# A new order of steps for a kernel whose TensorE plays attention and a gated network from one written list

## The chip, the cores and the metric

One core of a Trainium2 chip runs the whole program. The metric is the device time of one execution in microseconds; the time before is 1254.93, the median of three runs (1253.8 to 1256.23).

## The reference

The input x has 2048 tokens of 512 features. Two branches are computed from it and mixed by a gate for each token. All arrays are float32.

```python
g = sigmoid((x * gate_w).sum(-1, keepdims=True))

# branch A: attention, 32 query heads of 16, one shared key and value head
q = (x @ wq).reshape(B, S, 32, 16).transpose(0, 2, 1, 3)
k, v = x @ wk, x @ wv
p = softmax(einsum("bhqd,bkd->bhqk", q, k) * 16 ** -0.5)
a = einsum("bhqk,bkd->bhqd", p, v).transpose(0, 2, 1, 3).reshape(B, S, 512) @ wo

# branch B: a gated network of width 1376
b = (gelu(x @ w_gate) * (x @ w_up)) @ w_down

out = g * a + (1 - g) * b
```

## The kernel before

**Tiling.** The tokens are cut into 4 groups (`NTG`) of 512 (`TG`); the width 1376 into 11 chunks (`NF`) of up to 128; keys and values into 16 chunks (`NKC`) of 128 tokens. The 32 heads are handled in units of 4: a unit `u` is 4 heads for one group of 512 queries, so there are 32 units of 16 key chunks, 512 steps (`nsteps`). Two units make one block of heads, four blocks (`NB`) one group. Weights and activations are split into a high and a low part (names ending in h and l), and each product is made of three: high by high, low by high, high by low.

A first part, which the change doesn't touch, loads x, projects the queries (written to a scratch array `scr` in HBM and read back as `Q`), the keys (`kp`) and the values (`v1`, `v2`), and does the first chunks of the network. It ends about 82 us into the span.

**The list.** From there on TensorE's order is written out by hand. `PLAN` is a list of 78 strings, called entries here and counted from 0 (entry 0 stands on line 45). Each names a queue of jobs and a word of steps, and `play` emits them one after the other:

- `S`: `score`, one half of a step's scores. Two matmuls (L751) fill a pair of PSUM banks, and one exponential on ScalarE (L754) writes them to `p`, of which there are 12 (`PB`). There are three pairs of banks; `S` takes the one of the first two that was used longest ago, so it waits for the exponential that last read it. `Z` is the same step with the third pair, which it shares with the job's tile `z`.
- `V`: `visit`, one step of probabilities by values: eight matmuls in the trace (L821) into `acc`, from two tiles `p`. Behind the sixteenth V of a unit, `norm` is called: VectorE copies the sums (L765 or L775), and the normalization of a block (L781 to L799: two sums, a shuffle, four reciprocals, a product, and the split into `oh` and `ol`) is put into a list `bg`.
- `H`: begins a job; `z` and `y` are its two PSUM tiles. `F`: one pair of products, one for `z` and one for `y`, side by side on 64 rows each (L519). `R`: ends the job.
- `T`: queues the tanh of the job's GELU on ScalarE; the rest of the GELU follows on VectorE two and three scores later.

A job goes through its products twice, with the two halves of the rows exchanged in the second round; the hand-over from one half to the other waits for a small memset on GpSimd (`mark`, L527), which waits for the last products of the first half.

**The jobs.** Queue `f` holds the network's: a `gate_job` (12 products, so 24 F) makes gate and up projection of one chunk and starts its GELU; a `down_job` multiplies two or three chunks by `w_down` for two rows of 128 tokens and adds to `acc`. Behind the last chunk of a group, `reload_x` fetches x for the next one in four chunks; they are split when a slot in `pair_mm` comes up, and what is left is flushed when the next gate job begins (DVE casts on L201, GpSimd subtracts on L202). Queue `w` holds six output projections (`wo_job`): two for each of the first three groups, 12 products each, three for each of the four blocks of heads in order. When one begins, it flushes `bg`, so that the pending normalization is put into VectorE's queue:

```python
def begin():
    flush(lazy)
    flush(bg)
    return [[t for bl in range(NB) for t in wo_terms(g, k, bl)] for k in (i, i + 1)]
```

Each engine runs its own instructions in the order in which they were emitted and waits for the others by semaphores. `defer` and `run_later` tie the emission of small work (loads of Q, splits of weights) to the count of scores.

Of the kernel before, what the change touches and what calls it, by code (L numbers as in the profile page):

```python
# [20 lines left out]
S = 2048  # L21
D = 512
H = 32
DH = 16
F = 1376
# [16 lines left out]
EVERY = 3  # L42
PB = 12
PLAN = [
# [78 lines left out]
]  # L123


# [811 lines left out]
```

## Time and profile before

| | |
|---|---|
| median of three runs | 1254.93 us |
| the profiled execution | 1252.53 us |
| its span, first to last instruction | 1250.5 us |
| mean granted TensorE clock | 0.998 |
| ScalarE busy | 1033.1 us (83%) |
| VectorE busy | 521.1 us (42%) |
| GpSimd busy | 215.5 us (17%) |

TensorE's busy time counts overlapping matmuls up to their modelled ends, so it is near the whole span whether TensorE is fed well or not; the starts of its instructions tell more. Each instruction of the profile is named by its engine, its line, and its tiles, output before input: `acc<-p,v` reads `p` and `v` and writes `acc`. Engines are PE (TensorE), PEld (its weight loads), DVE (VectorE), ACT (ScalarE), POOL (GpSimd) and SP (which issues loads).

### The profile page before, as it was taken

Reading aid. Unit: us, or ns where it says so; the run is one execution under the profiler, and the core shown is the slowest. Engines: PE = TensorE matmul, PEld = TensorE weight load, DVE = VectorE, ACT = ScalarE, POOL = GpSimd, SP = SyncE. Lnnn points to the kernel's source line nnn. Section 1 sums busy time; section 2 is a strip of 40 time slices with the busy share of each in tenths; the row PEclk is TensorE's granted clock in tenths of the full one; section 3 lists DMA queues with packets and bytes.
Section 4 is the critical chain, followed back from the end, with each engine's and each line's share of the span. In section 5 each row is a group of like instructions: output and inputs, shape, how many; then the busy total and the mean of one; then the engine's idle time right before and its main releaser. Section 6 shows DMA issues by size and latency. Waiting matters only on the chain.

```text
span 1250.5 us, 23618 instructions
## 1 busy us (share of the span) xinstructions
PE 1240.0 (99%) x9742; PEld 657.4 (53%) x9742; DVE 521.1 (42%) x844; ACT 1033.1 (83%) x1127; POOL 215.5 (17%) x265
## 2 busy tenths in 40 slices
PE   9999999999999999999999999999998999999998
PEld 6865455454555554454455554455554555554444
DVE  7862453524423342533434253242635125253334
ACT  5448888889888889888988888987886888988894
POOL 5420312112210120211230021120331011121100
PEclk9999999999999999999999999999999999999999
DMA  8540302112200211201220111110220201011000
GB/s 328 194 153 38 94 1 65 40 48 82 73 15 24 75 40 40 65 23 47 74 72 19 57 65 40 40 40 23 85 82 14 73 14 65 14 52 40 14 1 34
DMA packets 28317, 73.89 MB, mean 59 GB/s; under 512 B 4208, under 2 KB 4464, under 8 KB 28208
## 3 DMA queue, kind: packets, MB, share of 16 engines
q1 hardware_dynamic: 27664, 71.32, 17.2%
q8 instruction: 77, 1.26, 0.4%
q0 software_dynamic: 256, 0.79, 0.2%
q10 hardware_dynamic: 288, 0.26, 0.1%
q14 instruction: 32, 0.26, 0.1%
HBM read 57.41 MB, written 14.94 MB: 58 GB/s over the span
## 4 chain that ended last, share of the span: by engine, by line
PE 92%; DVE 1%; DMA 0%; SPq 0%; ACT 0%; issue 0%; DVEq 0%
PE acc L821 38%; PE s L751 23%; PE y L519 16%; PE z L519 14%; PE wos L504 1%; DVE nz L787 0%; DMA Q<-scr 0%; DVE acc L634 0%; PE wof L504 0%; DVE sq L547 0%; DVE n L778 0%; DVE gs L555 0%; DVE sq L554 0%; DVE nt L790 0%; DVE sq L548 0%; DVE hl L560 0%
## 5 line engine op out<-in xcount | busy, mean ns | idle before, releaser
L754 ACT ACTIVATE p<-s 128x1024 f32<-128x1024 f32 x1024 | 979.8, 1025 | 157.5 <-PE s L751 142.7
L821 PE MATMUL acc<-p,v 128*32 128x512 f32 x4096 | 498.1, 600 | 0.0
L751 PE MATMUL s<-Q,kp 51*128 51x512 f32 x2048 | 396.9, 421 | 1.5 <-DMA Q<-scr 1.5
L751 PEld LDWEIGHTS s<-Q,kp 51*128 51x128 f32 x2048 | 183.4, 184 | 260.5 <-ACT p L754 158.4
L821 PEld LDWEIGHTS acc<-p,v 128*32 128x32 f32 x4096 | 107.3, 109 | 235.6 <-issue 224.0
L527 POOL MEMSET mark<- 1x1 f32 x77 | 7.7, 100 | 869.8 <-PE y L519 857.7
L544 DVE COPY gs<-z 128x512 f32<-128x512 f32 x39 | 27.0, 691 | 250.8 <-PE z L519 225.9
L519 PE MATMUL z<-xh,gh 64*128 64x512 f32 x312 | 123.2, 395 | 0.0
L519 PE MATMUL y<-xh,gh 64*128 64x512 f32 x312 | 123.1, 395 | 0.0
L519 PE MATMUL z<-xl,gh 64*128 64x512 f32 x312 | 121.9, 391 | 0.0
L519 PE MATMUL y<-xh,gl 64*128 64x512 f32 x312 | 121.9, 391 | 0.0
L519 PE MATMUL y<-xl,gh 64*128 64x512 f32 x312 | 121.9, 391 | 0.0
L519 PE MATMUL z<-xh,gl 64*128 64x512 f32 x312 | 121.9, 391 | 0.0
L202 POOL TENSOR_TENSOR gl<-st,gh 128x512 fp32r<-128x512 f32 x80 | 107.0, 1355 | 60.9 <-DVE gh L201 48.7
L624 DVE SCALAR_TENSOR_TENSOR acc<-z,gc,acc 128x512 f32<-128x512 f32 x24 | 18.0, 751 | 144.2 <-PE z L519 115.3
L519 PE MATMUL z<-dh,hh 64*128 64x512 f32 x176 | 69.4, 395 | 0.0
L519 PE MATMUL y<-dh,hh 64*128 64x512 f32 x176 | 69.4, 394 | 0.0
L519 PE MATMUL y<-dl,hh 64*128 64x512 f32 x176 | 68.9, 391 | 0.0
L519 PE MATMUL z<-dh,hl 64*128 64x512 f32 x176 | 68.8, 391 | 0.0
L519 PE MATMUL z<-dl,hh 64*128 64x512 f32 x176 | 68.8, 391 | 0.0
L519 PE MATMUL y<-dh,hl 64*128 64x512 f32 x176 | 68.8, 391 | 0.0
L519 PEld LDWEIGHTS z<-xh,gh 64*128 64x128 f32 x312 | 58.1, 186 | 8.1 <-issue 1.7
(174 smaller groups left out, 1534.8 us busy)
## 6 DMA issues: line engine op xcount, KB each, us to landing
st<-wf SPq DMA_DIRECT2D x40, 768.0 KB
scr<-q SPq DMA_DIRECT2D x16, 512.0 KB
Q<-scr SPq DMA_DIRECT2D x64, 128.0 KB
Q<-scr SPq DMA_DIRECT2D x64, 64.0 KB
out<-acc SPq DMA_DIRECT2D x16, 256.0 KB
xr<-xT SPq DMA_DIRECT2D x6, 512.0 KB
xst<-xT SPq DMA_DIRECT2D x12, 256.0 KB
st<-wf SPq DMA_DIRECT2D x5, 256.0 KB
```

The costliest lines, as they stand in the source:

```text
L202: eng_l.tensor_sub(lo, src, hi)
L504: nc.tensor.matmul(ps, a, b, start=(first and q == 0), stop=(last and q == len(terms) - 1), skip_group_check=True)
L519: mm = nc.tensor.matmul(ps, a[rs], b[rs], start=(half == 0 and q == 0), stop=(half == 1 and q == len(X) - 1), skip_group_check=True)
L527: relay = nc.gpsimd.memset(mark, 0.0).ins
L544: nc.vector.tensor_copy(gs, g)
L624: nc.vector.scalar_tensor_tensor(o, ps, w, o, op0=ALU.mult, op1=ALU.add)
L751: nc.tensor.matmul(ps[:, j * TG : (j + 1) * TG], kp[rs, kc * P : (kc + 1) * P], Q[u][rs, pr], start=True, stop=True)
L754: nc.scalar.activation(p, ps, AF.Exp, bias=0.0, scale=SCALE)
L821: nc.tensor.matmul(accp[u][32 * j : 32 * j + 32], vt[:, kc], pb[s, j // 2][:, (j % 2) * TG : (j % 2 + 1) * TG], start=(kc == 0), stop=(kc ...
```

## The change

Only the strings of `PLAN` differ. There are 78 entries before and after, with the jobs in the same order: the three pairs of output projections are entries 22 and 23, 41 and 42, 60 and 61 in both. Between them the numbers of scores, values and the places of `Z` and `T` are dealt out anew. The first entry, the entries around the output projections and the last ones, of 78 that nearly all differ:

```diff
 PLAN = [
-    "t: S",
-    "f: H F S F5 S F4 S F2 S V S F2 S F4 S F4 S F2 R S V Z S T S V3 S Z S V2 S",
...
-    "f: H F3 S F5 S F S V2 S2 F6 S F3 R S V S Z S V2",
-    "f: H F2 S F4 S F3 S V S F3 S F3 S F3 R S V2 Z S2 V3 S",
-    "w: H F2 S F4 S F3 S F3 S V S F2 S F4 S F3 S F3 R S V Z S2 V2 S Z V2 S2 Z V3 S",
-    "w: H F S F5 S F3 S F3 S V2 S2 F6 S F3 S F3 R S V2 Z S2 V2",
...
-    "f: H F5 S F S V S F3 S F3 R S V Z S2 V3 Z S2 V2 S",
-    "f: H F3 S F3 S V S F2 S F4 R S V S Z S V2 S",
-    "f: H F3 S F4 S F4 S F S V3 S2 F6 S F3 S F3 R S V S Z T S V2 Z S V2 S",
-    "f: H F4 S F2 S F6 S2 F6 S F5 S F R S V3 T Z S2 V2",
-    "f: H F S F2 S F4 S F2 S V S F3 S F3 S F3 R S V S Z S V3 S",
-    "w: H F S F5 S F6 S2 V3 S F3 S F3 S F4 S F2 R S V2 S Z S V2 S",
-    "w: H F3 S F4 S F2 S F3 S V4 S F S F5 S F3 S F3 R S V Z S2 V2 S",
...
-    "f: H F3 S F3 S F4 S F2 S V2 S F S F5 S F3 S F3 R S V3 T S Z S V2 S",
-    "w: H F4 S F4 S F2 S F2 V S F2 S F4 S F4 S F2 R S V S Z S V3 S Z S V3 S",
-    "w: H F S F5 S F3 S F3 S V3 S F2 S F4 S F4 S F2 R S V2 S2",
...
-    "f: H F3 S F3 S V S F2 S F4 R S V S Z S V2 S V3",
+    "t: S2",
+    "f: H F6 S F3 S F3 S V S F S F5 S F3 S F3 R S V S Z T S V2 Z S V2 S",
...
+    "f: H F3 S F3 S F3 S V S F2 S F4 S F3 R S V Z S2 V4 S Z S V2 S",
+    "f: H F3 S F5 S F S V S F3 S F3 S F3 R S V Z S2 V2 Z S V S Z V2 S2 Z V3 S",
+    "w: H F3 S F3 S F4 S F2 S V S F2 S F4 S F3 S F3 R S V Z S2 V3 S Z S V2 S",
+    "w: H F3 S F3 S F4 S F2 S V3 S F S F5 S F3 S F3 R S V Z S2 V3 S",
...
+    "f: H F3 S F3 S V S F S F5 R S V S Z S V2 S",
+    "f: H F4 S F2 S V S F6 R S2 V3 S",
+    "f: H F S F5 S F3 S F3 S V S F S F5 S F3 S F3 R S V Z S T S V4 S Z S V2 S",
+    "f: H F3 S F3 S F4 S F2 S V S F3 S F3 S F3 S F3 R S V Z S T S V4 Z S2 V2 S",
+    "f: H F3 S F5 S F S V S F3 S F3 S F3 R S V Z S2 V2 Z S V S Z V S2 V3 S",
+    "w: H F S F5 S F3 S F3 S V S F S F5 S F4 S F2 R S V2 S",
+    "w: H F S F5 S F4 S F2 S V4 S2 F6 S F3 S F3 R S V S Z S V2 S",
...
+    "f: H F4 S F3 S F5 S2 F6 S F3 S F3 R S V2 Z T S2 V4 S",
...
+    "f: H F2 S F4 S F4 S F2 S V S F3 S F3 S F3 S F3 R S V Z S V2 T S Z S V2 Z S V2 S Z S V2 S",
+    "w: H F3 S F3 S F3 S F3 S V S F S F5 S F5 S F R S V2 S Z S V4 S2",
+    "w: H F6 S F5 S F S V2 S2 F6 S F4 S F2 R S V2 S2",
...
+    "f: H F3 S F3 S V S F2 S F4 R S V Z S2 V2 S V3",
 ]
```

120 rows, old and new, of the table PLAN are left out of this document.

## The prediction

> **What bounds the kernel now.** I read the page first (busy shares, chain, groups), then the waits, then TensorE's timeline gap by gap.
>
> ```profile
> PE 1240.0 (99%) x9742; PEld 657.4 (53%) x9742; DVE 521.1 (42%) x844; ACT 1033.1 (83%) x1127; POOL 215.5 (17%) x265
> PE 92%; DVE 1%; DMA 0%; SPq 0%; ACT 0%; issue 0%; DVEq 0%
> L754 ACT ACTIVATE p<-s 128x1024 f32<-128x1024 f32 x1024 | 979.8, 1025 | 157.5 <-PE s L751 142.7 <-DMA Q<-scr 6.7 <-ACT p L754 1.1
> L751 PEld LDWEIGHTS s<-Q,kp 51*128 51x128 f32 x2048 | 183.4, 184 | 260.5 <-ACT p L754 158.4 <-issue 31.0 <-DVE gs L544 15.1
> ```
>
> TensorE is the bound: 92% of the chain that ended last. ScalarE has 157.5 us of idle time before its exponentials, most of it waiting for scores. The change only reorders TensorE's steps, so its price has two parts: what a step costs by its neighbours, and where TensorE waits. The prices, from the middle of the run (S = one score step, L751; F = one pair of products z and y, L519; V = one value step, L821, eight matmuls):
>
> ```profile
> 620.67 0.39 PE L519 MATMUL y<-dh,hl 64*128 64x512 f32 x1
> 620.90 0.40 PE L751 MATMUL s<-Q,kp 51*128 51x512 f32 x2
> 621.23 1.06 PE L821 MATMUL acc<-p,v 128*32 128x512 f32 x8
> 622.23 0.50 PE L751 MATMUL s<-Q,kp 51*128 51x512 f32 x2
> 622.57 0.39 PE L519 MATMUL y<-dh,hh 64*128 64x512 f32 x1
> 622.80 0.39 PE L519 MATMUL y<-dl,hh 64*128 64x512 f32 x1
> 623.03 0.40 PE L751 MATMUL s<-Q,kp 51*128 51x512 f32 x2
> 624.20 0.50 PE L751 MATMUL s<-Q,kp 51*128 51x512 f32 x2
> 624.63 1.07 PE L821 MATMUL acc<-p,v 128*32 128x512 f32 x8
> 626.51 1.92 PE L821 MATMUL acc<-p,v 128*32 128x512 f32 x16
> 628.37 0.50 PE L751 MATMUL s<-Q,kp 51*128 51x512 f32 x2
> ```
>
> From start to start: F to S, F to F and S to F 0.23; S to V 0.33 (620.90 to 621.23); one V 1.00, two 1.86 (626.51 to 628.37); the S behind a V 0.34.
>
> Where TensorE waits, there is one large place, at entry 60 of the list (counted from 0), the third pair of output projections. Its columns: start, length, engine, line, operation, and in brackets the idle time and what ended it.
>
> ```profile
> 951.06 0.39 PE L519 MATMUL z<-xh,gl 64*128 64x512 f32 x1
> 951.28 0.40 PE L751 MATMUL s<-Q,kp 51*128 51x512 f32 x2
> 951.61 2.78 PE L821 MATMUL acc<-p,v 128*32 128x512 f32 x24
> 954.33 0.96 PE L751 MATMUL s<-Q,kp 51*128 51x512 f32 x6
> 955.22 1.92 PE L821 MATMUL acc<-p,v 128*32 128x512 f32 x16
> 957.07 0.50 PE L751 MATMUL s<-Q,kp 51*128 51x512 f32 x2
> 959.74 0.40 PE L519 MATMUL y<-woh,ol 64*128 64x512 f32 x1
> 964.09 0.50 PE L519 MATMUL z<-woh,oh 64*128 64x512 f32 x1 [3.96 <-DVE oh L795]
> 967.11 0.79 PE L751 MATMUL s<-Q,kp 51*128 51x512 f32 x2
> 969.08 0.39 PE L519 MATMUL y<-woh,oh 64*128 64x512 f32 x1
> 951.49 0.69 DVE L544 COPY gs<-z 128x512 f32<-128x512 f32 x1 [1.10 <-PE z L519]
> 957.34 0.75 DVE L781 SCALAR_TENSOR_TENSOR nz<-n,mk,nz 128x512 f32<-128x512 f32 x1
> 963.61 0.43 DVE L795 CAST oh<-nt 128x512 fp32r<-128x512 f32 x1
> 961.00:964.00 3.00, 0.00 (x0) 0.00 (x0) 2.93 (x5) 0.02 (x1) 0.00 (x0) 1.00 0.00 0
> 965.30:968.60 3.30, 3.30 (x18) 1.34 (x18) 0.00 (x0) 1.25 (x2) 0.09 (x1) 0.50 0.00 0
> 969.00:972.00 3.00, 3.00 (x32) 2.17 (x30) 0.17 (x1) 2.65 (x4) 0.00 (x0) 1.00 0.00 0
> ```
>
> The tenth product of the job is the first that reads the last head block (oh, written by the cast at 963.61). It should start 0.23 behind 959.74, at 959.97, and starts at 964.09: 4.12 lost. In the windows (the seventh number behind the colon's stretch is the granted clock) TensorE does nothing from 961 to 964, and its clock then is 0.50 from 965.3 to 968.6 and 1.00 again from 969. The steps from 964.09 to 969.08, F S F F V S F F S F F, cost 3.28 by the prices above and took 4.99: another 1.7. So this one place costs 5.8 us.
>
> **The change part by part.** The job counts are equal: 1608 F, 1024 scores (904 S and 120 Z before, 905 and 119 after), 512 V, 77 jobs, 39 T. No instruction is added or removed; the part before the list and the tail behind it are untouched.
>
> *1. The wait at entry 60.* VectorE normalizes the block behind the GELU chain of entry 59's job, in the order of its queue, whatever TensorE does: from the copy at 951.49 to the end of the cast, 964.04. The new list keeps block 23's last V in the same place, in the middle of entry 59, but puts much more behind that entry's products. Before: S V3 S Z S V2 S, then 9 F and 2 S to the tenth product: 8.9 us from 951.06 to the 959.97 that it would be without the wait. After: S V Z S V2 S Z S V2 Z S V2 S Z S V2 S, then 9 F and 3 S. By the prices: V 1.00 + 4 x 1.86 = 8.44; twelve scores, five of 0.33 (in front of a V), five of 0.34 (behind one), and two of 0.23 in between, 3.81; 0.23 into the first; 12 x 0.233 = 2.8. Sum 15.3, so TensorE comes 6.4 later. VectorE comes later too: T, which queues the tanh, stands behind three scores instead of one, so two more exponentials can stand ahead of it on ScalarE.
>
> ```profile
> 623.12 2.86 ACT L754 ACTIVATE p<-s 128x1024 f32<-128x1024 f32 x3 [0.70 <-PE s L751]
> ```
>
> One exponential is 1.025 alone and three back to back 2.86, so (2.86 - 1.03)/2 = 0.915 each in a queue: 1.8 us for two. Wait left: 4.12 + 1.83 - 6.4 = -0.4, none. Without an idle stretch the clock stays at 1.00, so the 1.7 goes with it. Taken: -5.8. If VectorE is a microsecond later than I walk it, some 0.6 of wait stays and the clock stays up. Next late there: nothing on VectorE; the other two pairs (entries 22 and 41) had no wait, and 22 too gets more V in front.
>
> *2. Fewer turns to V.* Three V take 2.72 (951.61 to 954.33), so a V is worth 0.86 and a run of them 0.14 more; with 0.10 for the S to V step (0.33 against 0.23) and 0.11 for the S behind it, each run costs 0.35 over its V. Runs of one, two, three, four V: 112, 108, 48, 10 before (278), 106, 117, 36, 16 after (275). 3 x 0.35 = -1.0. The hand-overs between S and F go up from 1007 to 1015 and cost nothing, since both ways are 0.23.
>
> [...]
>
> *3. The score banks.* At 624.20 a score starts 0.05 behind the end of the first exponential of the row quoted (623.12 + 1.03 = 624.15), and the V behind it comes 0.43 later, not 0.33: its bank came free about 0.15 after the exponential's end. The same delay, read off the gaps, stands in 16 places by 0.05 to 0.10 each, 1.1 us in all, of which the first and the last are:
>
> ```profile
> 124.82 0.49 PE L751 MATMUL s<-Q,kp 51*128 51x512 f32 x2
> 125.23 1.07 PE L821 MATMUL acc<-p,v 128*32 128x512 f32 x8
> 1204.59 0.46 PE L751 MATMUL s<-Q,kp 51*128 51x512 f32 x2
> 1204.88 0.39 PE L519 MATMUL y<-xh,gl 64*128 64x512 f32 x1
> ```
>
> In the new list short gaps between scores get rarer: F runs of two and four (which alternate) go from 77 and 79 to 59 and 56, of three from 240 to 268. Walking both lists with 0.915 per exponential and a release at 0.15, I find about one such place left in the new one (entry 50, where the halves meet at S2). Bounds: 0 if they only move, -1.6 if smaller delays go as well. Taken: -1.0.
>
> *4. The second reload of x, entry 38.* One new wait. The casts of its third and fourth chunk are queued at the job's begin, and in the new list the copy of a finished block (L765) is queued just ahead.
>
> ```profile
> 622.36 0.69 DVE L765 COPY n<-acc 128x512 f32<-128x512 f32 x1 [5.92 <-PE acc L821]
> 622.97 0.42 DVE L201 CAST xh<-xst 128x512 fp32r<-128x512 f32 x1
> 623.47 1.30 POOL L202 TENSOR_TENSOR xl<-xst,xh 128x512 fp32r<-128x512 f32 x1 [2.19 <-DVE xh L201]
> 628.80 1.47 POOL L202 TENSOR_TENSOR xl<-xst,xh 128x512 fp32r<-128x512 f32 x1 [1.29 <-DVE xh L201]
> ```
>
> The copy starts 1.13 behind its V (621.23), in the new list 0.2 ahead of the job's first F (V to S 0.97, S to F 0.34). From that F at 0: copy to 0.5, cast, GpSimd's subtraction from 1.0 to 2.3, the second to 3.6 or 3.8. The eighth F reads the first at 9 x 0.233 = 2.1, the eleventh the second at 3.0: waits 0.2 and 0.4, sum +0.6. Bounds 0 (earlier casts) to +1.4 (both subtractions at 1.47, casts as late). GpSimd's mark for the halves queues behind these and is needed only after a V (0.9 or more); no cost. SP's loads are asked for by the same calls in the same order; 8 us lie between the last reload's issue and its use, and no row shows a wait of TensorE for them behind the first score.
>
> Sum: -5.8 - 1.0 - 1.0 + 0.6 = -7.2. The profiled execution took 1252.53 (span 1250.5 and 2.0 around it), which gives 1245.3; it lies 2.4 under the median of the three runs, so the forecast is 1254.93 - 7.2 = 1247.7.
>
> **The rivals.**
> - The wait at entry 60 only shrinks, because tanh, the added copy or a cast slowed by GpSimd push VectorE 2 us further: -7.2 + 2.0 = -5.2, 1249.7. For it: my margin is 0.4. Against: two exponentials is already the worst order. Chance 0.12.
> - The new list doesn't do there what it seems to: VectorE's chain follows TensorE, and the whole wait with the slow clock stays: -1.4, 1253.5, no change. Against: the cast at 963.61 ends a VectorE stretch that has no gap but the one for tanh. Chance 0.06.
> - [...] Chance 0.03.
> - Slower: ScalarE. In 13 jobs instead of 7 the tanh is followed by three scores at once. If there the queue is behind by one whole exponential beyond the release, the third score waits 0.915 for its bank each time: 13 x 0.915 = +11.9, so +4.7, 1259.6. It decides once ScalarE is over two exponentials behind at T. Against: before, at 954.33, three scores follow a T and take 0.89, the unhindered 0.34 + 0.23 + 0.33, and ScalarE idles 157.5 us. Chance 0.05.
>
> **How the numbers follow.** Forecast 0.74. Its ends: -5.8 - 1.3 - 1.6 + 0 = -8.7 and -4.1 (1.7 of the wait left) - 0.7 - 0 + 1.4 = -3.4, so 1246.2 to 1251.5; with 0.7 for the scatter of a median of three runs (they span 1253.8 to 1256.23), 1245.5 to 1252.2, which takes in the first and third rival and leaves 0.11 and the tails out. What a measurement of this kernel can tell from no change is about 0.2%, 2.5 us: faster 0.89 (forecast, first and third rival), same 0.06, slower 0.05.
>
> **What would show it.** In the profile after: no idle time of some 4 us for DVE oh among the waits; granted clock 1.00 through the whole list; 0.2 to 0.8 us of waiting for xl at about 623 to 625 us; V runs at the same 1.00, 1.86, 2.72; fewer S to V gaps over 0.40. Wrong if TensorE idles at entry 60, if a half-speed window appears elsewhere, or if scores behind T wait.

## The result, and the profile after

The new list takes 1247.15 us (median of six runs, 1245.13 to 1247.75) against 1254.28 for the old one measured beside it. The ratio is 0.9941 (95% interval 0.9928 to 0.9953), so 6 to 9 us less. The forecast was 7.2 us less, 1247.7. The profiled execution took 1246.9 with a span of 1244.8; before it was 1252.53 with 1250.5.

The page after, busy shares, chain and the two groups that answer to those of before:

```profile
PE 1237.2 (99%) x9742; PEld 657.5 (53%) x9742; DVE 526.2 (42%) x844; ACT 1031.7 (83%) x1127; POOL 215.6 (17%) x265
PE 92%; issue 1%; POOL 0%; DVE 0%; ACT 0%; DMA 0%; SPq 0%; POOLq 0%
L754 ACT ACTIVATE p<-s 128x1024 f32<-128x1024 f32 x1024 | 977.4, 1026 | 150.3 <-PE s L751 139.7
L751 PEld LDWEIGHTS s<-Q,kp 51*128 51x128 f32 x2048 | 183.7, 184 | 258.0 <-ACT p L754 167.3
```

Nothing in these lines tells where 6 us went: the shares are the same to a percent, and weight loads even wait longer for ScalarE in total (167.3 against 158.4), although the list is shorter. The timeline tells. At entry 60, the rows of TensorE and one of its weight loads, those of VectorE and ScalarE, and two windows:

```profile
952.09 0.39 PE L751 MATMUL s<-Q,kp 51*128 51x512 f32 x2
952.41 1.06 PE L821 MATMUL acc<-p,v 128*32 128x512 f32 x8
953.40 0.73 PE L751 MATMUL s<-Q,kp 51*128 51x512 f32 x4
966.59 0.39 PE L519 MATMUL z<-woh,ol 64*128 64x512 f32 x1
966.59 0.19 PEld L751 LDWEIGHTS s<-Q,kp 51*128 51x128 f32 x2
966.82 0.40 PE L751 MATMUL s<-Q,kp 51*128 51x512 f32 x2
967.05 0.39 PE L519 MATMUL z<-woh,oh 64*128 64x512 f32 x1
954.16 0.69 DVE L548 SCALAR_TENSOR_TENSOR sq<-sq,gs 128x512 f32<-128x512 f32 x1
956.50 0.69 DVE L554 SCALAR_TENSOR_TENSOR sq<-sq,gs 128x512 f32<-128x512 f32 x1 [1.65 <-ACT sq L551]
965.35 0.43 DVE L795 CAST oh<-nt 128x512 fp32r<-128x512 f32 x1
954.01 1.94 ACT L754 ACTIVATE p<-s 128x1024 f32<-128x1024 f32 x2 [0.41 <-PE s L751]
955.83 0.63 ACT L551 ACTIVATE sq<-sq 128x512 f32<-128x512 f32 x1
954.00:964.00 10.00, 10.00 (x84) 3.10 (x82) 8.11 (x14) 9.37 (x11) 0.00 (x0) 1.00 0.01 2
964.00:968.00 4.00, 4.00 (x34) 3.06 (x34) 2.40 (x4) 4.00 (x5) 0.00 (x0) 1.00 0.00 0
```

The cast that writes the last head block ends at 965.78; the tenth product starts at 967.05, when its turn comes, 1.27 us behind it. TensorE is busy in all of both windows and its clock is 1.00. A V alone costs 1.00 (952.41 to 953.40) and 0.32 lies between the score and it, as before.

At entry 38 TensorE's rows with those of VectorE and GpSimd behind them, and the wait as the waits view groups it (idle time of the weight loads: us in total, times, longest):

```profile
623.54 0.40 PE L519 MATMUL z<-xh,gh 64*128 64x512 f32 x1
625.42 0.40 PE L519 MATMUL z<-xh,gh 64*128 64x512 f32 x1
625.90 0.50 PE L519 MATMUL z<-xl,gh 64*128 64x512 f32 x1
626.25 0.39 PE L519 MATMUL z<-xh,gl 64*128 64x512 f32 x1
626.71 0.39 PE L519 MATMUL z<-xh,gh 64*128 64x512 f32 x1
627.33 0.50 PE L519 MATMUL z<-xl,gh 64*128 64x512 f32 x1 [0.24 <-POOL xl L202]
623.33 0.69 DVE L765 COPY n<-acc 128x512 f32<-128x512 f32 x1 [0.73 <-PE acc L821]
623.94 0.75 DVE L201 CAST xh<-xst 128x512 fp32r<-128x512 f32 x2
624.44 2.84 POOL L202 TENSOR_TENSOR xl<-xst,xh 128x512 fp32r<-128x512 f32 x2 [5.88 <-DVE xh L201]
PEld z L519 <- POOL xl L202: 1.2, 2, 0.7
```

The gaps are 0.48 and 0.62 where 0.23 is usual, and the step behind the first is 0.35 (625.90 to 626.25): the matmul that had waited also held up the next here, by 0.12.

The whole list, from its first score to the last run of V:

```profile
82.24 0.93 PE L751 MATMUL s<-Q,kp 51*128 51x512 f32 x4 [0.95 <-DMA Q<-scr]
1226.74 2.78 PE L821 MATMUL acc<-p,v 128*32 128x512 f32 x24
```

That is 1144.50 us, against 1150.87 before (81.61 to 1232.48): 6.4 less. The first score came 0.6 later in this profile, from before the list; over all profiled executions told of here it lies between 81.4 and 83.2, whatever the list.

### The profile page after: what moved, and what is told of

Its sections match the earlier page's. It is cut to its first block, busy times and chain, and to the rows that moved or that the text cites. A ratio compares the mean times of both kernels' runs of the same rounds, so it can differ in the third digit from the quotient of the medians.

```text
span 1244.8 us, 23618 instructions
## 1 busy us (share of the span) xinstructions
PE 1237.2 (99%) x9742; PEld 657.5 (53%) x9742; DVE 526.2 (42%) x844; ACT 1031.7 (83%) x1127; POOL 215.6 (17%) x265
## 4 chain that ended last, share of the span: by engine, by line
PE 92%; issue 1%; POOL 0%; DVE 0%; ACT 0%; DMA 0%; SPq 0%; POOLq 0%
PE acc L821 38%; PE s L751 23%; PE y L519 17%; PE z L519 13%; PE wos L504 1%; POOL xl L202 0%; DVE acc L634 0%; DMA Q<-scr 0%; PE wof L504 0%; ACT p L754 0%; SPq L364 0%; ACT sq L551 0%; SPq L363 0%; POOLq L202 0%; POOL mark L527 0%
## 5 line engine op out<-in xcount | busy, mean ns | idle before, releaser
L751 PEld LDWEIGHTS s<-Q,kp 51*128 51x128 f32 x2048 | 183.7, 184 | 258.0 <-ACT p L754 167.3
L519 PEld LDWEIGHTS y<-xh,gl 64*128 64x128 f32 x312 | 57.7, 185 | 8.4
```

The lines of the kernel that those rows point to most:

```text
L519: mm = nc.tensor.matmul(ps, a[rs], b[rs], start=(half == 0 and q == 0), stop=(half == 1 and q == len(X) - 1), skip_group_check=True)
L751: nc.tensor.matmul(ps[:, j * TG : (j + 1) * TG], kp[rs, kc * P : (kc + 1) * P], Q[u][rs, pr], start=True, stop=True)
```

## The experiments

The base of e1 and e2 is the old list, that of the others the new one. "List" is the time from the start of the first score to the start of the last V in the trace: 1152.6 before, 1146.2 after. Times in brackets are ranges of runs, ratios are to the old kernel. Distances to the new list are those of the medians; the ratios, made with other runs of the old kernel, give some 0.5 us more for e3, e5 and e6.

**e1, the wait alone, taken out of the old list**

```diff
-    "f: ... R S V3 T S Z S V2 S",
-    "w: H F4 S F4 ... F4 S F2 R S V S Z S V3 S Z S V3 S",
+    "f: ... R S V3 T S Z S V2 S Z S V S Z S V2 S",
+    "w: H F4 S F4 ... F4 S F2 R S V4 S",
```

> The list of before with one thing altered: three V and six scores move from behind entry 60's products to the end of entry 59, so that TensorE comes some 5 us later to the tenth product of the third output projection. Theory (the wait for the normalized block and the slow clock behind it are most of the gain): the wait of 4.1 us and the slow clock's 1.7 us go, three scores wait about 1.1 us in all for their exponentials because they stand closer, so -4.7 us against before, about 1249.6. Rival (the new order gains all along the list, and one wait removed is lost again further on): less than 1.5 us of gain.

1248.6 (1247.22 to 1248.83), ratio 0.9956 (0.9943 to 0.997): two entries of 78 bring 5.2 us. The list is 1147.9, 4.7 shorter; the tenth product starts 0.24 behind the ninth (966.11 to 966.35), 1.7 after the cast's end, and the clock stays at 1.00. The closer scores wait, much as expected, 1.2 in all over their usual gaps; the three largest are 0.69, 0.20 and 0.11.

```profile
959.84 0.91 PE L751 MATMUL s<-Q,kp 51*128 51x512 f32 x4
961.17 0.51 PE L751 MATMUL s<-Q,kp 51*128 51x512 f32 x2 [0.42 <-ACT p L754]
961.60 1.92 PE L821 MATMUL acc<-p,v 128*32 128x512 f32 x16
966.11 0.39 PE L519 MATMUL z<-woh,ol 64*128 64x512 f32 x1
966.35 0.40 PE L519 MATMUL z<-woh,oh 64*128 64x512 f32 x1
964.19 0.43 DVE L795 CAST oh<-nt 128x512 fp32r<-128x512 f32 x1
```

The rival of a gain spread over the list falls for these 5.2 us; the other 1.9 of the 7.1 lie elsewhere.

**e2, half of it**

```diff
-    "f: ... R S V3 T S Z S V2 S",
-    "w: ... R S V S Z S V3 S Z S V3 S",
+    "f: ... R S V3 T S Z S V2 S Z S V S",
+    "w: ... R S V S Z S V3 S V2",
```

> The list of before, with only three scores and one V moved ahead of entry 60's products. Theory: the wait shrinks from 4.1 to about 1.8 us, scores wait some 0.4 us more, and with an idle stretch that short the clock is not halved: -2.3 - 1.7 + 0.4 = -3.6 us, about 1250.7, with a granted clock of 1.00 in every window of the list. Rival (the clock falls after any wait of this kind): -1.9 us and a window at 0.50 behind the wait.

1249.47 (1248.65 to 1250.95), ratio 0.9966 (0.9955 to 0.9977): 4.35 less than the 1253.82 beside it, where 3.6 was expected. In the trace the list is 1149.7, only 2.9 shorter. The rows at the wait, with the cast, and the windows:

```profile
962.11 0.40 PE L519 MATMUL z<-woh,ol 64*128 64x512 f32 x1
964.09 0.50 PE L519 MATMUL z<-woh,oh 64*128 64x512 f32 x1 [1.58 <-DVE oh L795]
963.61 0.43 DVE L795 CAST oh<-nt 128x512 fp32r<-128x512 f32 x1
964.00:966.00 2.00, 1.91 (x16) 0.83 (x16) 0.73 (x2) 1.02 (x1) 0.09 (x1) 1.00 0.00 0
966.00:970.00 4.00, 4.00 (x36) 3.10 (x34) 0.00 (x0) 3.02 (x4) 0.00 (x0) 1.00 0.00 0
```

The wait is 1.98 - 0.23 = 1.75, and no window is at half speed. The cast still ends at the same time; only TensorE comes later, so VectorE's chain doesn't follow TensorE there. The 2.4 of waiting and the 1.7 of slow clock make 4.1; scores that stand closer take back 0.5, and one more run of V (279 for 278), which the expectation left out, some 0.3. What is left, 3.3, is near the 2.9 of the list and doesn't reach the 4.35 of the medians.

**e3, the wait put back into the new list**

```diff
-    "f: ... V2 T S Z S V2 Z S V2 S Z S V2 S",
-    "w: H F3 S F3 S F3 S F3 S V S F S F5 S F5 S F R S V2 S Z S V4 S2",
+    "f: ... V2 T S Z S V2 S",
+    "w: H F3 S F3 S F3 S F3 S V2 S F S F5 S F5 S F R S V2 S Z S V2 Z S V2 S Z S V3 S2",
```

> The new list with the distance taken out again: four V and five scores move from the end of entry 59 into entry 60, the rest of the list is the new one. Theory: TensorE waits 4.0 to 4.6 us at the tenth product, its clock falls to 0.50 for 3.4 us, which costs another 1.7: +5.7 to +6.3 us against the new list, 1253 to 1253.5, all but 1 us of what the change gained. Rival (the gain is spread over the list): within 1.5 us of the new list's 1247.

1252.54 (1251.38 to 1254.05), ratio 0.9989 (0.998 to 0.9998): 5.4 above the new list, a little under the 5.7 expected, and most of the gain is gone. Its profiled execution, which took 1253.98, 1.4 above the median:

```profile
961.92 0.40 PE L751 MATMUL s<-Q,kp 51*128 51x512 f32 x2
966.19 0.79 PE L519 MATMUL z<-woh,oh 64*128 64x512 f32 x1 [3.87 <-DVE oh L795]
968.20 3.64 PE L821 MATMUL acc<-p,v 128*32 128x512 f32 x16
971.77 0.50 PE L751 MATMUL s<-Q,kp 51*128 51x512 f32 x2
965.00:966.10 1.10, 0.00 (x0) 0.00 (x0) 1.07 (x2) 0.00 (x0) 0.00 (x0) 0.50 0.00 0
966.20:971.70 5.50, 5.50 (x24) 1.71 (x24) 0.66 (x1) 1.02 (x1) 0.09 (x1) 0.50 0.00 0
971.90:974.00 2.10, 2.10 (x20) 1.76 (x22) 0.00 (x0) 1.63 (x2) 0.00 (x0) 1.00 0.00 0
```

The wait is 4.27 - 0.23 = 4.04, as in the old list. The half speed begins during the wait here and lasts until 971.7 or a little later; two V take 3.57 (968.20 to 971.77) instead of 1.86. The list is 1152.9, 6.7 longer: 4.0 of waiting and 2.7 of slow clock, where the old list's profile had 1.7 for it. With 1.7 the sum would be 5.7, nearer to the medians' 5.4.

**e5, eighteen more runs of V.** For instance, in 18 entries, with the counts of each entry kept:

```diff
-    "f: ... T S V4 S Z S V2 S",
+    "f: ... T S V2 S Z V2 S V2 S",
```

> The new list with longer runs of V cut by a score that stood next to them, in 18 entries: 293 runs of V instead of 275, the same numbers of scores, products and V in each entry. Theory (a run of V costs 0.33 to 0.35 us over its V, wherever it stands): +6.0 to +6.3 us against the new list, 1253.1 to 1253.5, with the same 1.00, 1.86 and 2.72 for runs of one, two and three. Rival (turning from scores to V is hidden by the weight loads pulled ahead): under 1.5 us. Rival (ScalarE is served more evenly by cut runs and TensorE waits less): a gain.

1253.02 (1251.19 to 1253.85), ratio 0.9993 (0.9984 to 1.0002): 5.9 above the new list, and the list is 1152.1, 5.8 longer, 0.32 a run. One of them:

```profile
136.31 0.51 PE L751 MATMUL s<-Q,kp 51*128 51x512 f32 x2
136.75 1.92 PE L821 MATMUL acc<-p,v 128*32 128x512 f32 x16
138.60 0.50 PE L751 MATMUL s<-Q,kp 51*128 51x512 f32 x2
138.94 0.39 PE L519 MATMUL z<-xh,gh 64*128 64x512 f32 x1
```

Two V are 1.85 in a cut run too, with 0.34 behind the score that follows. The lone score between two runs takes 0.44 to the V behind it: 0.23, with 0.11 for standing behind a V and 0.10 for standing in front of one. A turn to V isn't hidden, and the gain that the second rival hoped for by way of ScalarE doesn't show.

**e6, eleven entries with scores two products earlier**

```diff
-    "f: H F3 S F3 S F3 S F3 ...",
+    "f: H F S F3 S F5 S F3 ...",
```

> The new list with two scores of a gate job's first half put two products earlier (F S F3 S F5 S F3 for F3 S F3 S F3 S F3) in 11 entries; counts are unaltered. Theory (a bank of scores is free for TensorE only 0.15 us after its exponential's end, and the list gains by keeping that distance): the second score or its follower waits about 0.29 us in each of the 11 entries: +3.0 us against the new list, about 1250. If the release came at 0.05, +1.9. Rival (scores are held by nothing in these stretches, ScalarE has idle time to spare): under 0.5 us.

Ten of the entries hold gate jobs and one, entry 60, an output projection. 1250.41 (1250.17 to 1251.36), ratio 0.9971 (0.996 to 0.9981): 3.3 above the new list, and the list is 1149.7, 3.4 longer. At entry 31:

```profile
530.76 0.40 PE L519 MATMUL z<-xh,gh 64*128 64x512 f32 x1
531.19 0.50 PE L751 MATMUL s<-Q,kp 51*128 51x512 f32 x2
531.54 0.39 PE L519 MATMUL y<-xl,gh 64*128 64x512 f32 x1
```

0.43 and 0.35 where 0.23 is usual: 0.32. This fits the total of 0.15 behind the exponential's end, and not one of 0.05, which would give 0.19. What the 0.15 is made of stays open: the score's record starts 0.05 behind the exponential's end (531.14) and the rest falls on the step behind it, as at entry 38, where TensorE had waited for GpSimd and not for a bank. In stretches of products the scores do stand just where ScalarE lets them.

**e4, the new wait taken away**

```diff
-                    slot(half == 1 or q + 6 <= len(X))
+                    slot(half == 1 or q + 6 <= len(X) or (len(X) == 6 and q == 5))
```

> The new list, unaltered; in the code that hands out small work during products, jobs of six products (those that lie behind a reload of x) may split a chunk of x at the sixth product of their first half too, so that all four chunks are split before the next gate job begins. Theory (entry 38 waits for the subtractions of the last two chunks because they are put into the queues only when the job begins): the two waits there, 0.4 + 0.25 us and their after-effects, go: -0.6 to -0.9 us against the new list, about 1246.4. Rival (the waits are the loads' from HBM, or VectorE is simply full there): no gain, or the wait moves to the copies ahead of it.

1246.45 (1245.96 to 1247.02), ratio 0.9939 (0.9926 to 0.9953). Against the new list's 0.9941 that is no difference a measurement can tell; the trace tells it. All four chunks are split before the job begins, two by two, and the products run at their usual gap:

```profile
608.87 2.52 POOL L202 TENSOR_TENSOR xl<-xst,xh 128x512 fp32r<-128x512 f32 x2
618.21 2.53 POOL L202 TENSOR_TENSOR xl<-xst,xh 128x512 fp32r<-128x512 f32 x2
626.35 0.40 PE L519 MATMUL z<-xh,gh 64*128 64x512 f32 x1
626.58 0.40 PE L519 MATMUL z<-xl,gh 64*128 64x512 f32 x1
```

The list is 1145.6, 0.7 less, the shortest of all the lists, by a step that only the trace shows.

## Why the prediction was right, point by point

- **The wait at entry 60 (-5.8).** Right, and for the reason given. The distance on TensorE's side came out as walked: from entry 59's last product (0.23 ahead of the score at 952.09) to the tenth at 967.05 it is 15.2, for 15.3 by the prices. VectorE's side was mis-sized: the tanh was to come up to 1.8 later, and starts 0.98 after its input (954.16 + 0.69 = 954.85, against 955.83): two exponentials do stand ahead of it, but the first started at 954.01, 0.84 before the input was ready. So the spare time is 1.27 instead of 0.4, and neither rival that kept some or all of the wait came true. e1 and e3 show the term from both sides: 5.2 us gained by removing the wait from the old list although 1.2 of new score waits came in, and 5.4 lost by putting it back into the new one.
- **Fewer runs of V (-1.0).** Right. With the gap from each step to the next set to the median of such gaps in the old trace (same step before, same two steps), the old list sums to 1143.7 and the new one to 1142.7, 1.0 less. e5 gives 0.32 a run for the 0.35 that I used.
- **The hand-overs between S and F (third rival, chance 0.03).** Falls. The rival added a price for the eight more hand-overs to the forecast's sum, and no run shows such a price. At entry 60 (966.59, 966.82, 967.05) F to S and S to F are 0.23 as before, and the loads for the score at 966.82 run from 966.59 to 966.78, under the product that starts at 966.59.
- **The score banks (-1.0).** Right in kind and a little too large. Gaps over their median by more than 0.015, without entry 60, the opening and entry 38, exceed it by 1.7 in all before and 1.0 after: -0.7. The walk left one such place, entry 50; in the trace entries 14, 32, 42 and 70 have one of 0.08 to 0.11 too. e6 shows the mechanism and the 0.15 in total.
- **The reload of x (+0.6).** Right place and cause, mis-sized: 0.25 and 0.39 of waiting plus 0.11 for the step behind each, 0.86, where the old list lost 0.1. The waits are as forecast (0.2 and 0.4); the step missing in my sum was this restart. e4 shows the cause.
- **Not in the sum.** The many small deviations under 0.015 add 0.4. So the list's 6.4 is 5.8 + 1.0 + 0.7 - 0.8 - 0.4 = 6.3, the rest being rounding.
- **The number.** That the medians differ by 7.1 where 7.2 was forecast is in part luck. The sum was worked out from the old list's profiled execution, and from that it asks for 1245.3; the new list's profiled execution took 1246.9, and profile against profile the change is 5.6. The old list's median in the result is 1.75 above its profiled execution (1254.28 against 1252.53), the new list's 0.25 (1247.15 against 1246.9). The clock's price, which seems to differ from run to run (last section), may be part of that; no trace of a longer run of the old list shows it.
- **ScalarE behind T (rival, +4.7 in all).** Did not happen: none of the 13 places has a gap over its median by more than 0.02. The mechanism exists, though: in e1, where three scores stand behind two V and three more behind the next one V, the last of them waits 0.7 for an exponential.

## What to carry to other kernels

When the bound engine is 99% busy by the page, look at the starts of its instructions: a single wait and the clock it costs were about three quarters of what a list of 78 new entries gained (5.2 and 5.4 of 7.1, by e1 and e3), and changing two entries of the old list brings most of it. Price a reordering by hand-overs, count them in both orders, and then walk each wait's two sides separately; a consumer that stands later helps even if its producer is late too, as long as the producer's queue doesn't follow the consumer. Before trusting a new order, look for the queue that is filled only when a job begins: in e4 one slot handed out earlier removed its wait without touching the order, though its 0.7 us is too little for the medians to show.

## What the runs showed of the hardware

The clock's price wasn't fixed by the length of the wait. In the profiled executions a wait of 1.75 us left the clock alone (e2); waits of 4.12 (before) and 4.04 (e3) halved it, but once from 965.3 to 968.6, behind the wait, at 1.7 us, and once from within the wait, at 965.0, to 971.7, about twice as long (6.7 us against 3.3), at 2.7 us. So two waits of nearly the same length cost differently; what decides between the two the traces don't show.

The runs of the old list point the same way. Of the 23 measured beside e1, e2, e3 and e5, 15 have a mean granted clock of 0.997 and 8 of 0.999, and the first have spans 1.5 us longer on average (1252.2 against 1250.8); of the 12 beside e4 and e6, 3 have 0.997 and 8 have 0.999, and the difference is 1.0 us (1252.5 against 1251.6). The profiled execution had 0.998, and the new list's six runs 0.999 to 1.0. So one and the same list seems to pay more in some runs than in others; the mean also takes in the end of the span, so it doesn't tell how many stretches a run had.
